# A later place for ScalarE's evacuation of the product with V, and a power of two moved into the exponential's bias

## The chip, the cores and the metric

The kernel runs on one core of a Trainium2 chip. The metric is the device time of one execution in microseconds. Times are compared by medians of runs; the rows below come from one profiled execution.

## The reference

The program computes pooled attention and then an MLP with a layer norm, in float32. q, k and v have 4 batches, 8 heads, 1152 positions and 64 columns. Pairs of query positions are averaged, so there are 576 queries per head.

```
q_pool = q.reshape(B, H, S // 2, 2, D).mean(axis=3)
scores = scale * q_pool @ k.T;  scores -= max(scores)
attn = exp(scores);  attn /= sum(attn) + 1e-9
x = attn @ v            # heads side by side: (4, 576, 512)
xn = (x - mean) / sqrt(var + 1e-6) * g_ln
out = x + max(xn @ w_ch1, 0) @ w_ch2
```

## The kernel before

**Tiles and steps.** Two heads of one batch make a pair; there are 16 pairs. Each pair has 9 tiles of 128 queries (the fifth holds 64 queries of either head), so there are 144 steps, one tile of 128 queries by 1152 keys each. The steps are written out by hand, in `step(i)`; every engine runs its instructions in the order in which they are written there. In the first 36 steps (`on_pe`) the exponentials are transposed by TensorE (PE) in float32. In the other 108, which the change is about, they are split into an fp16 high and low half and transposed by a DMA.

**A step i of the second kind**, in the order of writing:

- `emit_max(i)`: VectorE (DVE) takes the row maximum of the scores from PSUM (L381) and makes the bias `nb` of the exponential from it (L386).
- `emit_s(i + 1)`: PE computes the scores of the next tile (L362, and L370 for the last 128 keys). A tile of scores takes three PSUM banks, a slot; two slots alternate. L370 writes the third bank of a slot.
- `flush()`: what was put on the list `evacs` in the step before. First the two parts of `evac_pv`, which evacuate the product with V: `one` is DVE's sum and reciprocal `r` (L513, L514), `two` is ScalarE's (ACT's) scaled copy into the tile `xb` or `xh` (L524). Then the evacuation of the MLP unit (ACT's high half of `ht`, L618, and DVE's low half, L619; or DVE's residual add, L650), of the layer norm's transposes (L574, L575), and the high and low halves of the next pair's k and q (L286 or L311, and L283 or L306).
- `emit_exp(i)` and `emit_hi(i)`: ACT's exponential from PSUM into the SBUF tile `pe` (L395), and its high half into `hl` (L409), with the factor 2^15. Three buffers of `hl` are in turn; one is free again when its transposing DMA is done.
- `emit_lo(i - 1)`: the low half, (2^15 pe - hi), by DVE (L418), or for tiles 2, 5 and 8 of a pair (`low_on_pool`) by GpSimd (POOL) with one pass that scales `pe` in place (L251) and one that subtracts (L416). Then the DMA that transposes `hl` into `pt` (L421), on the queue of SP.
- `norm(i)`: the layer norm of a finished block of 128 rows: DVE's statistics (L550, L551) and POOL's scaling (L556 to L562).
- `a_piece(i)`: PE's product with V of a tile four steps back (L464). It goes into columns 128 to 257 of the third bank of the slot whose first 128 columns hold the last scores of step i + 1. Its evacuation is put on `evacs`.
- `some_units(i)`: one unit of the MLP, if there is one: PE's L605 (first matmul) or L637 (second). `a_prep`: one transpose of k or q for the next pair (L297, L301 or L325). Further transposes are those of the layer norm (L568). All of these take one of two PSUM banks from `bank()`. If neither is free, `bank()` calls `flush()` early, in the middle of the step.
- the end of the step: loads, ACT's Abs passes over k, q and v (`bound`, L185) in the second and third step of a pair, from whose sums PE, DVE and GpSimd make the scales of the next pair in the two steps after (`all_max`, `scales`).

After step 143 the MLP units that are left run on PE, two a step.

Of the kernel before, what the change touches and what calls it, by code (L numbers as in the profile page):

```python
# [2 lines left out]

# [10 lines left out]
ACTF = mybir.ActivationFunctionType  # L14
ALU = mybir.AluOpType
# [9 lines left out]
def tile_pooled_attention_moe(  # L25
# [18 lines left out]
    nc = tc.nc  # L44
# [4 lines left out]
    C = S // 128  # L49
# [178 lines left out]
    def scales(p, top, a=0, b=3, both=False):  # L228
        st = pair[p]
        red, e, s, sc = (st[x] for x in ("red", "e", "s", "sc"))  # L230
        v = nc.vector
        v.tensor_scalar(red[:, a:b], top, TINY, None, op0=ALU.max)
        if both:

            v.tensor_tensor(red[:, 0:1], red[:, 0:1], red[:, 2:3], op=ALU.max)
        ri, ei, si = (x.bitcast(I32)[:, a:b] for x in (red, e, s))
        v.tensor_scalar(ei, ri, EXPO, None, op0=ALU.bitwise_and)
        v.tensor_scalar(si, ri, EXPO, EXPO, op0=ALU.bitwise_and, op1=ALU.bitwise_xor)

        v.tensor_scalar(s[:, a:b], s[:, a:b], 2.0 ** 13, None, op0=ALU.mult)  # L240
        if a == 0:
            v.scalar_tensor_tensor(
                sc[:, 0:1], e[:, 0:1], 2.0 ** -32, e[:, 1:2], op0=ALU.mult, op1=ALU.mult
            )
            if on_pe(p * C):
                v.scalar_tensor_tensor(
                    sc[:, 1:2], e[:, 0:1], -(2.0 ** -32), e[:, 1:2], op0=ALU.mult, op1=ALU.mult
                )

    def scaled(dst, src, s=1.0):  # L250
        nc.gpsimd.tensor_scalar(dst, src, s, 1.0, op0=ALU.mult, op1=ALU.mult)  # L251
# [84 lines left out]
    def on_pe(i):  # L336

        return 0 <= i < HP * C

    def low_on_pool(i):  # L340
        return i % C in (2, 5, 8)
# [35 lines left out]
    def emit_max(i):  # L377
        st = steps[i]
        mx = sm_p.tile([128, 1], FP32, tag="mx", name="mx")
        nb = st["nb"] = sm_p.tile([128, 1], FP32, tag="nb", name="nb")  # L380
        nc.vector.tensor_reduce(mx, st["s"], axis=AX.X, op=ALU.max)  # L381
        sc = pair[i // C]["sc"]
        if on_pe(i):
            st["mx"] = mx
        else:
            nc.vector.tensor_scalar(nb, mx, sc[:, 0:1], -1.0, op0=ALU.mult, op1=ALU.mult)  # L386

    def emit_exp(i):
        st = steps[i]
# [16 lines left out]
    def emit_hi(i):  # L406
        st = steps[i]
        hl = st["hl"] = p_p.tile([128, 2, S], FP16, tag="hl", name="hl", bufs=3)
        nc.scalar.activation(out=hl[:, 0], in_=st["pe"], func=ACTF.Copy, scale=2.0 ** 15)  # L409

    def emit_lo(i):
        st = steps[i]
        hl = st["hl"]
        if low_on_pool(i):
            scaled(st["pe"], st["pe"], 2.0 ** 15)
            nc.gpsimd.tensor_tensor(hl[:, 1], st["pe"], hl[:, 0], op=ALU.subtract)  # L416
        else:
            nc.vector.scalar_tensor_tensor(  # L418
                hl[:, 1], st["pe"], 2.0 ** 15, hl[:, 0], op0=ALU.mult, op1=ALU.subtract
            )  # L420
        nc.sync.dma_start_transpose(out=pt_of(i), in_=hl.rearrange("p a n -> p (a n)"))  # L421
# [65 lines left out]
    def evac_pv(i, ps):  # L487

        p, j = divmod(i, C)
        b, hp = divmod(p, HP)  # L490
        s = pair[p]["s"][:, 2:3]
        r = sm_p.tile([128, 2], FP32, tag="r", name="r", bufs=3)
        if j == 4:
            if b % 2 == 0 and hp == 0:
                xh[b // 2] = x_p.tile([128, 2, DM], FP32, tag="hh", name="xh")
            o, n, m = 64 * (b % 2), 64, 2
            x = xh[b // 2][o:o + n, 0, 128 * hp:128 * hp + 128]
        else:
            if j == 0 and hp == 0:
                room["x"] -= 4  # L500
                assert room["x"] >= 0
                xb[b] = x_p.tile([128, 4, DM], FP32, tag="xb", name="xb")
            h, t = PLACES[hp // 2][j]
            o, n, m = 0, 128, 1
            x = xb[b][:, t, 128 * hp + 64 * h:128 * hp + 64 * h + 64]
        r = r[o:o + n, 0:m]

        def one():
            sums = ps[o:o + n, 64:65 * m:65]
            if on_pe(i):  # L510
                nc.vector.reciprocal(r, sums)
            else:
                nc.vector.tensor_scalar(r, sums, EPS, s[o:o + n], op0=ALU.add, op1=ALU.mult)  # L513
                nc.vector.reciprocal(r, r)  # L514

        def two():
            for u in range(m):
                if on_pe(i):
                    nc.vector.tensor_scalar(
                        x[:, 64 * u:64 * u + 64], ps[o:o + n, 65 * u:65 * u + 64],  # L520
                        r[:, u:u + 1], None, op0=ALU.mult,
                    )
                    continue
                nc.scalar.activation(  # L524
                    out=x[:, 64 * u:64 * u + 64], in_=ps[o:o + n, 65 * u:65 * u + 64],
                    func=ACTF.Copy, scale=r[:, u:u + 1],
                )

        return one, two
# [47 lines left out]


    units, preps = deque(), deque()
    evacs = []  # L580

    def flush():
        mine, evacs[:] = list(evacs), []
# [333 lines left out]
    def evacuated(n):  # L917

        p, j = divmod(n, C)
        b = p // HP  # L920
        left[p] -= 1
        if not left[p]:
            pair.pop(p)
        key = ("h", b // 2) if j == 4 else (b, PLACES[p % HP // 2][j][1])
        whole[key] = whole.get(key, 0) + 1
        if whole[key] == 8 and key != ("h", 0):
            norms.append(key)
# [17 lines left out]
    def a_piece(i):  # L945
        pieces.extend(ready.pop(i, ()))
        for u in range(2 if len(pieces) > 2 and not on_pe(i) else 1):
            if pieces:
                n = pieces.popleft()
                pt = pts[n]  # L950
                ps = emit_pv(n, bank() if u or on_pe(n) else None)
                if on_pe(n):
                    ot = pt.rearrange("p a n -> p (a n)").bitcast(FP32)[0:65, 0:128]
                    evacs.append(lambda ot=ot, ps=ps: nc.scalar.activation(
                        out=ot, in_=ps[0:65, 0:128], func=ACTF.Identity, bias=eps
                    ))
                    turned.append((n, ot))
                    continue
                evacs.extend(evac_pv(n, ps))
                evacs.append(lambda n=n: evacuated(n))  # L960

    def step(i):
        live = i < NSTEP
        this[0] = i
        for fn, a in early.pop(i, ()):
            fn(*a)
        if live:
            emit_max(i)
        if on_pe(i - 1):
            emit_t_copy(i - 1)  # L970
            steps.pop(i - 1)
        while found:
            found.popleft()()
        first = on_pe(i - 2) or on_pe(i)
        if first and not on_pe(i):
            a_piece(i)
        if on_pe(i):
            if i < 3:
                warm(16, bank())
            a_piece(i)  # L980
            a_prep()
            emit_exp(i)
        while scaled_out:
            scaled_out.popleft()()
        if i + 1 < NSTEP:
            emit_s(i + 1)
            pv_slot[0] = i + 1
        else:
            free_banks[:] = [6, 7, 0, 1, 3, 4]
            pv_slot[0] += 1  # L990
        if on_pe(i):
            while fill:
                drip()
            flush()
        else:
            flush()
            if live:
                emit_exp(i)
                emit_hi(i)
        if 0 <= i - 1 < NSTEP and not on_pe(i - 1):  # L1000
            emit_lo(i - 1)
            steps.pop(i - 1)
            drip()
        norm(i)
        while soon or len(fill) > 3:
            drip()
        if on_pe(i):
            emit_t(i)
            if reds:
                found.append(reds.popleft()())  # L1010
        elif reds:
            evacs.append(reds.popleft()())
        while turned:
            n, ot = turned.popleft()
            emit_turn(n, ot, i)
        if not on_pe(i):
            if not first:
                a_piece(i)
            some_units(i)
            a_prep()  # L1020
        for fn, a in todo.pop(i, ()):
            fn(*a)
        if calm and i < HP * C - 1:
            gate()
        for _ in range(1 if i < HP * C - 1 else 2):
            if calm:
                fn, n = calm.popleft()
                fn(n)
# [6 lines left out]
    with tc.manual_schedule():  # L1035
# [17 lines left out]
        st = state(0)  # L1053
# [29 lines left out]
        i = 0  # L1083
# [32 lines left out]
```

## Time and profile before

| what | value |
|---|---|
| runs | 865.6, 866.25, 870.39 us; median 866.25 |
| profiled execution | 860.85 us, its span 859.0 us |
| PE, DVE, ACT, POOL busy | 810.0, 604.2, 561.8, 349.5 us |
| TensorE's granted clock over the span | 0.996 of full speed |

The span is the time from the first to the last instruction of the profiled execution. Busy times are sums over it. A row of a timeline has the start of an instruction in us from the span's start, its duration in us, the engine, the line, the output and input by the program's names, and in brackets how long the engine had been idle and what ended that.

### The profile page before, as it was taken

The page shows a single profiled execution, that of the slowest core. Times are in us where ns is not written, and L with a number is a line of the kernel's source. Part 1 is how long each engine was busy: PE and PEld are TensorE (multiplying, and loading weights), DVE is VectorE, ACT ScalarE, POOL GpSimd, SP SyncE. Part 2 cuts the span into 40 slices and gives each one's busy share as a digit, 9 for nine tenths or more (in the row PEclk, how much of TensorE's full clock was granted, in tenths as well). Part 3 has the DMA queues.
Part 4 walks back from the last instruction along what each step waited for, and adds up shares of the span by engine and source line. Part 5 has one row for each costly group of instructions (what it writes and reads, how often), then busy time and mean ns, then how long its engine had stood idle before and what let it go on. Part 6 is the DMA issues. An engine that isn't in the chain of part 4 may idle for free.

```text
span 859.0 us, 21617 instructions
## 1 busy us (share of the span) xinstructions
PE 810.0 (94%) x9142; PEld 574.4 (67%) x9142; DVE 604.2 (70%) x1166; ACT 561.8 (65%) x810; POOL 349.5 (41%) x345
## 2 busy tenths in 40 slices
PE   7999999988889998998999999999999999999997
PEld 6787877766556665656575766666666666766764
DVE  4698899898778877788777777777777777531221
ACT  3999988867676767677686867676867676311110
POOL 3020333487888845436534244634542514300000
PEclk9999999999999999999999999999999999999999
DMA  6853465025695869887898989776989968500001
GB/s 178 223 206 122 158 179 182 1 63 107 134 203 110 175 124 223 147 166 141 156 180 158 174 146 203 146 153 123 217 143 158 171 117 139 100 10 20 19 2 24
DMA packets 276016, 115.95 MB, mean 135 GB/s; under 512 B 259280, under 2 KB 259280, under 8 KB 275920
## 3 DMA queue, kind: packets, MB, share of 16 engines
q1 hardware_dynamic: 275568, 113.70, 64.5%
q8 instruction: 71, 1.16, 0.6%
q10 hardware_dynamic: 352, 0.88, 0.4%
q14 instruction: 25, 0.20, 0.1%
HBM read 46.14 MB, written 4.72 MB: 59 GB/s over the span
## 4 chain that ended last, share of the span: by engine, by line
PE 45%; DVE 27%; ACT 12%; DMA 8%; issue 4%; POOL 2%; SPq 2%; ACTq 0%; POOLq 0%; DVEq 0%
PE psum L637 14%; PE psum L605 14%; DVE mx L381 8%; DVE hl L418 6%; PE psum L464 5%; PE psum L362 4%; ACT pe L395 3%; DMA qr<-in_q_dram 2%; DMA kr<-in_k_dram 2%; DVE ht L619 2%; PE psum L452 2%; ACT ht L618 2%; DMA pt<-hl 2%; DVE kt L283 2%; PE psum L428 2%
## 5 line engine op out<-in xcount | busy, mean ns | idle before, releaser
L381 DVE TENSOR_REDUCE mx<-psum 128x1 f32<-128x1152 f32 x144 | 194.7, 1352 | 19.3 <-ACT xb L524 7.4
L637 PE MATMUL psum<-wsl,ht 128*128 128x512 f16 x864 | 196.6, 379 | 5.1 <-DVE ht L619 4.3
L395 ACT ACTIVATE pe<-psum,nb,sc 128x1152 f32<-128x1152 f32 x144 | 188.8, 1311 | 11.8 <-DVE nb L386 10.4
L605 PEld LDWEIGHTS <-wsl 128*128 128x128 f16 x1920 | 170.2, 98 | 28.2 <-issue 9.6
L605 PE MATMUL psum<-xn,wsl 128*128 128x256 f16 x1536 | 178.1, 274 | 8.8 <-DVE xb L650 5.9
L637 PEld LDWEIGHTS <-ht 128*128 128x128 f16 x864 | 80.8, 98 | 93.6 <-issue 5.8
L409 ACT ACTIVATE hl<-pe 128x1152 f16<-128x1152 f32 x108 | 125.6, 1163 | 9.5 <-DMA pt<-hl 6.2
L362 PE MATMUL psum<-kt,qt 64*128 64x512 f16 (+1 forms) x960 | 127.3, 380 | 1.9 <-ACT pe L395 0.9
L619 DVE SCALAR_TENSOR_TENSOR ht<-psum,ht 128x512 f16<-128x512 f32 x72 | 49.8, 692 | 100.7 <-ACT ht L618 100.7
L464 PE MATMUL psum<-vt,pt 128*128 128x65 f16 (+1 forms) x3240 | 118.4, 194 | 0.2 <-DMA pt<-hl 0.2
L418 DVE SCALAR_TENSOR_TENSOR hl<-pe,hl 128x1152 f16<-128x1152 f32 x72 | 112.1, 1556 | 0.0
L464 PEld LDWEIGHTS <-pt 128*128 128x128 f16 (+1 forms) x3240 | 110.1, 101 | 2.8 <-DMA pt<-hl 0.7
L618 ACT ACTIVATE ht<-psum 128x512 f16<-128x512 f32 x72 | 42.7, 593 | 87.0 <-PE psum L605 86.6
L251 POOL TENSOR_SCALAR pe<-pe 128x1152 f32<-128x1152 f32 x36 | 43.1, 1198 | 130.5 <-ACT hl L409 130.5
L524 ACT ACTIVATE xb<-psum,r 128x64 f32<-128x64 f32 x96 | 29.9, 311 | 93.8 <-DVE r L514 80.6
L416 POOL TENSOR_TENSOR hl<-pe,hl 128x1152 f16<-128x1152 f32 x36 | 85.5, 2374 | 3.0
L452 PE MATMUL psum<-pt,vt 128*65 128x128 f32 (+1 forms) x720 | 77.4, 263 | 1.1 <-DVE qt L283 1.1
L452 PEld LDWEIGHTS psum<-pt,vt 128*65 128x65 f32 x720 | 71.5, 138 | 1.3 <-DVE qt L283 1.3
L362 PEld LDWEIGHTS <-qt 64*128 64x128 f16 (+1 forms) x960 | 39.7, 96 | 39.6 <-issue 22.1
L370 PEld LDWEIGHTS <-qt 128*128 128x128 f16 (+1 forms) x320 | 17.0, 99 | 61.5 <-issue 61.4
L283 DVE SCALAR_TENSOR_TENSOR qt<-psum,s,qt 128x384 f16<-128x384 f32 x48 | 29.5, 615 | 31.1 <-ACT qt L286 31.0
L257 POOL COPY gate<-gate 128x1 f32<-128x1 f32 x27 | 5.2, 193 | 110.5 <-DVE gate L256 110.5
(116 smaller groups left out, 1010.8 us busy)
## 6 DMA issues: line engine op xcount, KB each, us to landing
stage<-in_moe_w_ch_dram SPq DMA_DIRECT2D x32, 512.0 KB, 5.9
kr<-in_k_dram SPq DMA_DIRECT2D x16, 576.0 KB, 4.6
qr<-in_q_dram SPq DMA_DIRECT2D x31, 288.0 KB, 6.1
vr<-in_v_dram SPq DMA_DIRECT2D x15, 576.0 KB, 5.0
out_dram<-xb SPq DMA_DIRECT2D x32, 128.0 KB, 2.4
pt<-hl SPq DMA_TRANSPOSE x108, 4.9
kr<-in_k_dram SPq DMA_DIRECT2D x16, 64.0 KB, 4.2
vr<-in_v_dram ACTq DMA_DIRECT2D x1, 576.0 KB, 6.5
```

Source lines behind the costliest of these rows:

```text
L362: nc.tensor.matmul(out=sp[o:o + w, c0:c0 + 512], lhsT=qt[r:r + 64, qa, q0:q0 + w], rhs=kt[r:r + 64, ka, h], start=(a == 0), stop=(a == 2),)
L381: nc.vector.tensor_reduce(mx, st["s"], axis=AX.X, op=ALU.max)
L395: nc.scalar.activation(out=st["pe"], in_=st["s"], func=ACTF.Exp, scale=pair[i // C]["sc"][:, 0:1], bias=st["nb"],)
L409: nc.scalar.activation(out=hl[:, 0], in_=st["pe"], func=ACTF.Copy, scale=2.0 ** 15)
L416: nc.gpsimd.tensor_tensor(hl[:, 1], st["pe"], hl[:, 0], op=ALU.subtract)
L418: nc.vector.scalar_tensor_tensor(hl[:, 1], st["pe"], 2.0 ** 15, hl[:, 0], op0=ALU.mult, op1=ALU.subtract)
L452: nc.tensor.matmul(out=ps[0:65, q0:q0 + w], lhsT=vt[:, h, c], rhs=pt[:, 128 * u + q0:128 * u + q0 + w], start=(u == 0), stop=(u == C - 1),)
L464: nc.tensor.matmul(out=dst[:, 0:n], lhsT=lhsT, rhs=rhs, start=(u == 0 and lhsT is hi and n == 65), stop=(u == C - 1 and lhsT is lo), skip_ ...
L605: nc.tensor.matmul(out=ps[:, o:o + n], lhsT=wsl[:, 8 * w + cc, wa, f * 128:f * 128 + 128], rhs=xn[:, xa * KD + cc, 0:n], start=(m == 0), s ...
L618: lambda: nc.scalar.activation(out=hi, in_=pv, func=ACTF.Relu),
L619: lambda: nc.vector.scalar_tensor_tensor(lo, pv, 0.0, hi, op0=ALU.max, op1=ALU.subtract),
L637: nc.tensor.matmul(out=ps, lhsT=hv[0][:, ha, f, t * 128:t * 128 + 128], rhs=wsl[:, 8 * w + 4 + f // 2, wa, (f % 2) * DM:(f % 2) * DM + DM] ...
```

## The change

Three edits. The second part of the evacuation of the product with V (L524) is no longer put on `evacs` but on a list of its own, `last`. A step takes that list at its start and runs it behind the exponential and the high half, ahead of the low half; the first part stays on `evacs`. Second, for GpSimd's tiles the bias of the exponential gets 15 log 2 added, so that `pe` itself is 2^15 times as large; the high half is then taken with the factor 1, and GpSimd's pass that scaled `pe` is left out. Third, `nb` is made with the negative product of the scales and an addition, so `scales` makes that product for every pair and not only for the first four.

```diff
--- before.py
+++ after.py
@@ -1,3 +1,4 @@
+import math
 from collections import deque
 from contextlib import ExitStack
 
@@ -242,10 +243,9 @@
             v.scalar_tensor_tensor(
                 sc[:, 0:1], e[:, 0:1], 2.0 ** -32, e[:, 1:2], op0=ALU.mult, op1=ALU.mult
             )
-            if on_pe(p * C):
-                v.scalar_tensor_tensor(
-                    sc[:, 1:2], e[:, 0:1], -(2.0 ** -32), e[:, 1:2], op0=ALU.mult, op1=ALU.mult
-                )
+            v.scalar_tensor_tensor(
+                sc[:, 1:2], e[:, 0:1], -(2.0 ** -32), e[:, 1:2], op0=ALU.mult, op1=ALU.mult
+            )
 
     def scaled(dst, src, s=1.0):
         nc.gpsimd.tensor_scalar(dst, src, s, 1.0, op0=ALU.mult, op1=ALU.mult)
@@ -383,7 +383,8 @@
         if on_pe(i):
             st["mx"] = mx
         else:
-            nc.vector.tensor_scalar(nb, mx, sc[:, 0:1], -1.0, op0=ALU.mult, op1=ALU.mult)
+            up = 15 * math.log(2) if low_on_pool(i) else 0.0
+            nc.vector.tensor_scalar(nb, mx, sc[:, 1:2], up, op0=ALU.mult, op1=ALU.add)
 
     def emit_exp(i):
         st = steps[i]
@@ -406,13 +407,13 @@
     def emit_hi(i):
         st = steps[i]
         hl = st["hl"] = p_p.tile([128, 2, S], FP16, tag="hl", name="hl", bufs=3)
-        nc.scalar.activation(out=hl[:, 0], in_=st["pe"], func=ACTF.Copy, scale=2.0 ** 15)
+        up = 1.0 if low_on_pool(i) else 2.0 ** 15
+        nc.scalar.activation(out=hl[:, 0], in_=st["pe"], func=ACTF.Copy, scale=up)
 
     def emit_lo(i):
         st = steps[i]
         hl = st["hl"]
         if low_on_pool(i):
-            scaled(st["pe"], st["pe"], 2.0 ** 15)
             nc.gpsimd.tensor_tensor(hl[:, 1], st["pe"], hl[:, 0], op=ALU.subtract)
         else:
             nc.vector.scalar_tensor_tensor(
@@ -577,7 +578,7 @@
 
 
     units, preps = deque(), deque()
-    evacs = []
+    evacs, last = [], []
 
     def flush():
         mine, evacs[:] = list(evacs), []
@@ -956,8 +957,9 @@
                     ))
                     turned.append((n, ot))
                     continue
-                evacs.extend(evac_pv(n, ps))
-                evacs.append(lambda n=n: evacuated(n))
+                one, two = evac_pv(n, ps)
+                evacs.append(one)
+                last.extend((two, lambda n=n: evacuated(n)))
 
     def step(i):
         live = i < NSTEP
@@ -972,6 +974,7 @@
         while found:
             found.popleft()()
         first = on_pe(i - 2) or on_pe(i)
+        final, last[:] = list(last), []
         if first and not on_pe(i):
             a_piece(i)
         if on_pe(i):
@@ -997,6 +1000,8 @@
             if live:
                 emit_exp(i)
                 emit_hi(i)
+        for fn in final:
+            fn()
         if 0 <= i - 1 < NSTEP and not on_pe(i - 1):
             emit_lo(i - 1)
             steps.pop(i - 1)
```

## Rows read from the trace of the kernel before

**Rows 1.** The page, busy us of the engines, share of the span, instructions

```profile
PE 810.0 (94%) x9142; PEld 574.4 (67%) x9142; DVE 604.2 (70%) x1166; ACT 561.8 (65%) x810; POOL 349.5 (41%) x345
```

**Rows 2.** The page, chain of work that ended last, by engine

```profile
PE 45%; DVE 27%; ACT 12%; DMA 8%; issue 4%; POOL 2%; SPq 2%; ACTq 0%; POOLq 0%; DVEq 0%
```

**Rows 3.** Busy us by stretch: length, PE, PEld, DVE, ACT, POOL, clock, DMA

```profile
220.00:400.00 180.00, 161.49 (x1996) 107.34 (x1996) 139.03 (x244) 126.13 (x169) 115.16 (x93) 0.98 0.84 162
400.00:740.00 340.00, 330.92 (x4193) 224.12 (x4190) 257.49 (x470) 242.86 (x322) 144.57 (x130) 1.00 0.86 156
```

**Rows 4.** Instructions of L409: ns min/median/max, first and last start

```profile
L409 ACT ACTIVATE hl<-pe x108: 1162/1163/1166, 186.3 to 734.5; 128x1152 f16<-128x1152 f32 x108
```

**Rows 5.** Waits of PE: us in total, times, longest

```profile
PE psum L605 <- DVE xb L650: 5.9, 4, 2.1
PE psum L637 <- DVE ht L619: 4.3, 5, 1.0
PE psum L605 <- DVE ht L619: 2.9, 4, 1.7
...
PE psum L370 <- DVE xb L519: 0.7, 2, 0.4
```

**Rows 6.** Waits of the other engines: us in total, times, longest

```profile
DVE ht L619 <- ACT ht L618: 100.7, 71, 3.4
...
ACT xb L524 <- DVE r L514: 80.6, 65, 5.9
...
DVE mx L381 <- ACT xb L524: 7.4, 11, 1.7
...
ACT hl L409 <- DMA pt<-hl: 6.2, 7, 2.8
```

**Rows 7.** Timeline of a step: start, us, engine, line, names [idle before, releaser]

```profile
450.84 0.38 PE L301 MATMUL psum<-ident,kr 128*128 128x128 f32 x2
...
451.84 0.21 DVE L513 TENSOR_SCALAR r<-psum,s 128x1 f32<-128x1 f32 x1
...
452.03 0.98 PE L464 MATMUL psum<-vt,pt 128*128 128x65 f16 x27
...
452.35 0.32 ACT L524 ACTIVATE xb<-psum,r 128x64 f32<-128x64 f32 x1 [1.92 <-DVE r L514]
452.56 0.59 ACT L618 ACTIVATE ht<-psum 128x512 f16<-128x512 f32 x1
...
453.18 0.69 DVE L619 SCALAR_TENSOR_TENSOR ht<-psum,ht 128x512 f16<-128x512 f32 x1 [0.93 <-ACT ht L618]
...
453.92 2.75 PE L637 MATMUL psum<-wsl,ht 128*128 128x512 f16 x12 [0.91 <-DVE ht L619]
```

**Rows 8.** Timeline from 272 to 300 us, where DVE is late

```profile
283.57 0.51 ACT L524 ACTIVATE xh<-psum,r 64x64 f32<-64x64 f32 x2 [3.43 <-DVE r L514]
...
284.72 0.62 DVE L283 SCALAR_TENSOR_TENSOR qt<-psum,s,qt 128x384 f16<-128x384 f32 x1 [1.25 <-ACT qt L286]
...
293.21 2.78 PE L605 MATMUL psum<-xn,wsl 128*128 128x256 f16 x24 [1.90 <-DVE xb L650]
```

**Rows 9.** Timeline from 308 to 345 us, a high half that waits for its buffer

```profile
334.39 0.28 PE L370 MATMUL psum<-kt,qt 128*128 128x128 f16 x2
...
334.95 1.16 ACT L409 ACTIVATE hl<-pe 128x1152 f16<-128x1152 f32 x1 [2.83 <-DMA pt<-hl]
```

**Rows 10.** L418 and GpSimd's passes: groups of the page, then ns min/median/max

```profile
L418 DVE SCALAR_TENSOR_TENSOR hl<-pe,hl 128x1152 f16<-128x1152 f32 x72 | 112.1, 1556 | 0.0
...
L251 POOL TENSOR_SCALAR pe<-pe 128x1152 f32<-128x1152 f32 x36 | 43.1, 1198 | 130.5 <-ACT hl L409 130.5
...
L418 DVE SCALAR_TENSOR_TENSOR hl<-pe,hl x72: 1347/1350/3510, 189.3 to 733.9; 128x1152 f16<-128x1152 f32 x72
...
L251 POOL TENSOR_SCALAR pe<-pe x36: 1149/1153/2248, 199.8 to 737.9; 128x1152 f32<-128x1152 f32 x36
```

## Prediction

> **What bounds the kernel now.** I read the page's busy times first: PE is busy 810.0 us of a span of 859.0 [rows 1], so all idle time of PE is worth 49 us at most. The chain that ended last says where it lies: 45% PE, 27% DVE, 12% ACT [rows 2]; DVE's queue often released what came last, even where PE had other work. The busy times by stretch narrow it: from 220 to 400 us PE is idle 18.5 us of 180, from 400 to 740 us 9.1 us of 340 [rows 3]. The steps that the change touches run their high half from 186.3 to 734.5 us, 108 of them [rows 4], so about 30 us of PE idle lie inside its reach, and most of the second stretch is pure PE.
>
> The list of what PE waited for tells which idle it is [rows 5]: 4.3 us ahead of the second MLP matmul and 2.9 us ahead of the first, both for the low half of `ht` (L619) that frees a PSUM bank; 5.9 us for the residual add L650. On the other engines [rows 6]: DVE sat idle 100.7 us, 71 times (1.42 us each), ahead of L619 for the high half of `ht` from ACT, and ACT sat idle 80.6 us, 65 times, ahead of the evacuation `xb` (L524) for the reciprocal of DVE. These two are one story, and one step shows it [rows 7]: the MLP unit's matmuls are over when the transposes of L301 begin, 450.84. ACT stands idle 1.92 us, because the next in its queue is `xb`, which needs `r`, which stands on DVE behind the maximum and `nb`. Only after `xb` (452.35) come `ht` (452.56) and the kt copy; so DVE gets to L619 at 453.18, and PE, through with its product with V at 452.03 + 0.98 = 453.01, waits 0.91 us until 453.92.
>
> **The change, part by part.**
>
> *`xb` behind the high half.* In such a step ACT now runs `ht` as soon as the unit's matmuls are over, about 450.9 to 451.5, and kt after it. DVE has `r` at 451.84 + 0.21 and the reciprocal some 0.2 us later, about 452.25, and goes straight into L619, 0.69 us, to 452.94. That is before 453.01, so the 0.91 us go whole. Nine waits of PE are of this kind (7.2 us, rows 5). Eight of them end on the step's order, and I take all of them; in the ninth, the largest of L605 (1.67 us, the first step after the change of scheme), the scale work ahead of `r` stays and 0.9 us go. Sum: 7.2 - 0.8 = 6.4 us.
>
> The DVE chain gets shorter too. At 283.57 ACT had waited 3.43 us for `r` ahead of the evacuation; the copy of the queries was queued behind it, and DVE stood 1.25 us for that copy. DVE is late in that stretch, and PE pays at 293.21 with 1.90 us for L650 [rows 8]. There I take 1.2 us, DVE's whole wait. The other waits for L650 start from a maximum that waits for its scores or behind a stretched low half; 1.0 us of them in all, mostly because the maximum no longer waits for `xb` where an early flush puts `xb` ahead of it (7.4 us, 11 times, rows 6). Together 2.2 us.
>
> What pays: (a) behind `xb` ACT runs the Abs passes L185 in two steps of each pair, and PE waits for these. ACT does the same work in another order; where it was saturated nothing changes, where a high half waits for its buffer the passes come 0.3 us later. I take 0.3 us once; bounds 0 and 12 pairs x 0.3 = 3.6. (b) The layer norm's statistics read `xb`. In nine steps they now stand on DVE until the high half and `xb` are through, up to 1.2 us each, and the next maximum is queued behind them. PE has no gap behind them in those steps, and DVE has idle time in the next; I take 0, bounds 0 and 9 x 0.5 = 4.5. (c) A new wait: the scores of step i+2 write the third bank of the slot that `xb` reads (L370), so PE there waits for exp, high half and `xb` and no longer for exp alone. Behind L370 are queued the product with V and the next unit. Normally L370 begins 0.7 us or more after the high half's end; where the high half waits for its buffer (6.2 us, 7 times, rows 6) it doesn't: at 334.95 it starts after 2.83 us of waiting, ends 336.11, and with 0.31 of `xb` L370 goes from 334.39 to some 336.45 [rows 9]. Just behind it PE has one of its waits for L650, which swallows most; 0.3 us left there, 0.2 us at a second such place. Bounds: 0, and the worst case of the slower rival below.
>
> Is that wait real, since `xb` and L370 touch different columns? The rows speak for it: the maximum, which reads other columns of the bank, waited for `xb` [rows 6], and L370 waited twice for a DVE evacuation, 0.7 us [rows 5]. By the same rows exp keeps waiting for `r`, whose sum DVE reads from the bank, and not for `nb` alone; so I count no gain for exp itself. The Trainium skill (PSUM — Partial Sum Buffer, "PSUM bank collisions raise a hardware error") speaks against the change here: two engines must not be in one bank on the same partitions at once, reads against reads included, and the guard goes by bank, not by address. By that rule L370 stands behind `xb` in all 108 steps, which is the slower rival's mechanism; if waits went by columns, (c) would cost nothing and the sum be -8.0 us. The trace agrees as far as these two rows go.
>
> *2^15 through the bias.* 36 passes of GpSimd go, 1198 ns on average, 43.1 us; its subtraction can start when ACT's high half ends, so the low half and its transposes come 1.2 us earlier. PE hardly waits for any transposed tile in these steps, so nothing on the path. What could gain is DVE: its low half takes 1347 ns at the least and 3510 at the most, 112.1 us for 72, so 15 us of stretch [rows 10], which lies beside GpSimd's work. The passes are 43.1 of GpSimd's 349.5 us [rows 1]: 12% of 15 is 1.8 us. They seldom meet the low half, though: a median of 1153 against a mean of 1198 ns is 1.6 us of stretch over all 36 passes. I take 0, bounds -1.8, and +1.8 if the subtraction, now earlier, meets more of DVE's work. The bias itself goes into an instruction that is there (`nb`, mult and add in place of two mults), and ACT's scale is 1 in place of 2^15: 0.
>
> *One more scale product in 12 pairs*: of the size of `r`, 0.21 us [rows 7], and queued ahead of it: 2.5 us if all on the path; PE is mostly busy there, 0.3 taken.
>
> **Sum**: -6.4 - 2.2 + 0.3 + 0.5 + 0.3 = -7.5 us. The profiled execution took 860.85 us, of which 1.85 lie around the span: 853.4. The median of the runs is 866.25, 5.4 higher; the same step from there gives 858.7.
>
> **Rivals.**
>
> *The gaps only move.* PE is busy 97% of the second stretch; a step that is ready sooner meets the next limit (the maximum behind a late low half, the loads of q and k). For it: the waits for L650 that start from a late maximum, for L185's sums and for the layer norm's transposes stay where they are. Against: PE has 9.1 us of idle time in the whole second stretch, so few waits are there to take it back. If half is given back: -3.5, 862.7.
>
> *DVE sets more of the pace than I count.* It has 27% of the chain, and loses most of 100.7 us of waiting. Then the rest of the waits for L650 (5.9 less 2.2) and a like amount of the other idle time before 400 us go as well: 7 us more, -14.5, 851.7. Against: from 400 us on only 9.1 us are there to be had.
>
> *Slower, by the third bank.* L370 held behind high half and `xb` is one mechanism; it decides where the high half ends later than L370's start less 0.4 us. If all seven buffer waits fall through to PE they cost 6.2 + 7 x (1.16 + 0.31) = 16.5 us, and only the gaps behind them cover it: +16.5 - 8 = +8.5 at worst, +6 taken, 872. For it: 334.95 [rows 9]. Against: the other six waits share 3.4 us, and L370 stands later there.
>
> *It doesn't do what it says*: where the unit is unfinished when DVE has `r`, the order of the two makes no difference. That happens in other steps, not in the nine counted; it ends with the first rival.
>
> **Chances.** Forecast 0.55 (its own range 853 to 862, as the bounds will not all fall on one side); gaps move or nothing happens 0.23; DVE's pace 0.13; slower 0.09. This kernel's runs lie within 0.6%, so 0.5% (4.3 us) is about what can be told from no change: faster 0.68, same 0.23, slower 0.09. The range, 849 to 866, leaves out the slower rival and the far end of the faster one.
>
> **What would show it.** The wait of `xb` for the reciprocal gone from ACT's list, L619's wait for `ht` well under 100 us; PE's waits for L619 ahead of L605 and L637 near zero; the maximum never waiting for `xb`. A new row "L370 waits for `xb`" would show (c): under 3 us in sum if I am right, over 8 if the slower rival is. The statistics L550 should wait for `xb`. GpSimd busy about 306 us, and the low half's longest times as before. I am wrong if those waits go and PE's idle from 220 to 740 us stays near 27 us, or if it falls under 15.

## The result, and the profile after

The changed kernel took 852.79 us (median of 6 runs, 847.55 to 857.0), the kernel before 864.66 beside it (862.87 to 870.39): a ratio of 0.9861, 95% interval 0.9819 to 0.9903. In a second measurement it was 850.92 against 863.46, ratio 0.9866 (0.9833 to 0.9899). So the change gains 1.3 to 1.4%, some 12 us; forecast were 7.5. The sign and the range hold, the size is 4 to 5 us short.

The time of one kernel goes with the mean granted clock of its run: 846.89 us at 1.0 and 855.91 at 0.989 in the second measurement, 858.78 at 1.0 and 867.62 at 0.989 for the kernel before. The first profiled run of the changed kernel was its slowest (857.0, clock 0.990). All lines of the changed kernel below are therefore from the profiled run of the second measurement (849.85, span 848.1, clock 0.995). Lines behind the edits stand one or two lower than before: L201 is now L202, L409 is L411, L418 L419, L524 L525, L568 L569, L605 L606, L618 and L619 are L619 and L620, L637 L638, L650 L651.

The page of that run: the busy times, and the chain of work that ended last, by engine.

```profile
PE 808.2 (95%) x9142; PEld 574.1 (68%) x9142; DVE 606.1 (71%) x1178; ACT 558.1 (66%) x810; POOL 308.5 (36%) x309
...
PE 64%; ACT 11%; DVE 11%; DMA 6%; issue 4%; SPq 1%; POOL 1%; ACTq 0%; POOLq 0%; DVEq 0%
```

DVE gained 12 small instructions (the scale products) and stayed as busy; GpSimd lost its 36 passes, 41 us. The chain changed from 45% PE and 27% DVE [rows 1, 2] to 64% and 11% (63% and 11% in the first profiled run): DVE's queue seldom releases the work that came last any more.

Busy times by stretch, columns as in [rows 3], with GB/s behind the DMA share:

```profile
220.00:400.00 180.00, 164.84 (x2077) 110.92 (x2078) 146.19 (x258) 129.15 (x173) 104.98 (x85) 0.98 0.86 165
400.00:735.00 335.00, 329.17 (x4174) 222.69 (x4172) 255.52 (x474) 236.88 (x321) 117.22 (x107) 1.00 0.87 160
```

PE's idle time from 220 us on is 15.2 + 5.8 = 21.0 us, against 18.5 + 9.1 = 27.6 [rows 3]. I had called the forecast wrong if it stayed near 27 or fell under 15. In the first profiled run, at its lower clock, the two stretches hold 15.7 + 8.3 = 24.0 us. Over the whole span idle time went from 859.0 - 810.0 = 49.0 to 848.1 - 808.2 = 39.9 us.

PE's waits, us in total, times, longest:

```profile
PE psum L202 <- ACT kt L186: 6.4, 6, 2.0
...
PE psum L569 <- DVE ht L620: 4.1, 4, 1.1
PE psum L370 <- ACT xb L525: 3.3, 5, 1.4
...
PE psum L606 <- DVE xb L651: 2.3, 2, 1.9
...
PE psum L606 <- DVE ht L620: 0.7, 1, 0.7
```

And those of the other engines that answer to [rows 6]:

```profile
ACT ht L619 <- PE psum L606: 131.9, 59, 12.4
DVE ht L620 <- ACT ht L619: 86.4, 59, 3.5
...
ACT pe L396 <- DVE r L514: 9.8, 10, 2.2
...
ACT hl L411 <- DMA pt<-hl: 9.6, 11, 2.4
...
DVE bs L551 <- ACT xb L525: 8.5, 9, 1.9
...
ACT xb L525 <- DVE r L515: 8.1, 2, 4.6
```

The second MLP matmul (L638) no longer waits for anything that the list shows; the first waits once for `ht`. ACT's 80.6 us ahead of `xb` are 8.1, in two places. The maximum never waits for `xb`. What appeared is what the forecast named: exp waits for `r`, L370 for `xb`, the statistics L551 for `xb`. One sign came only in part: L620 still waits 86.4 us of 100.7 for `ht`, since `ht`, no longer behind `xb`, now waits for its own matmul in more places (131.9 us, 59 times; 86.6, 29 times before).

The step of [rows 7], 7.0 us earlier on this kernel's clock:

```profile
443.81 0.38 PE L301 MATMUL psum<-ident,kr 128*128 128x128 f32 x2
444.00 0.60 ACT L619 ACTIVATE ht<-psum 128x512 f16<-128x512 f32 x1 [1.07 <-PE psum L606]
...
444.66 0.21 DVE L514 TENSOR_SCALAR r<-psum,s 128x1 f32<-128x1 f32 x1
...
444.98 0.67 DVE L620 SCALAR_TENSOR_TENSOR ht<-psum,ht 128x512 f16<-128x512 f32 x1
445.00 0.98 PE L465 MATMUL psum<-vt,pt 128*128 128x65 f16 x27
...
445.81 2.75 PE L638 MATMUL psum<-wsl,ht 128*128 128x512 f16 x12
...
447.31 0.30 ACT L525 ACTIVATE xb<-psum,r 128x64 f32<-128x64 f32 x1
```

`ht` now waits for its own matmul (1.07 us) and for nothing else; `xb` comes 3.3 us after it. From the transposes L301 to the second MLP matmul it takes 445.81 - 443.81 = 2.00 us, where it took 453.92 - 450.84 = 3.08 [rows 7]: 1.08 us less, forecast 0.91. The low half L620 starts when PE starts its product with V, and ends before that does.

### The profile page after: what moved, and what is told of

The parts are those of the page before. It is cut to its first block, busy times and chain, and to the rows that moved or that the text cites. A ratio compares the mean times of both kernels' runs of the same rounds, so it can differ in the third digit from the quotient of the medians.

```text
span 855.2 us, 21585 instructions
## 1 busy us (share of the span) xinstructions
PE 811.9 (95%) x9142; PEld 577.1 (67%) x9142; DVE 603.0 (71%) x1178; ACT 558.8 (65%) x810; POOL 308.5 (36%) x309
## 4 chain that ended last, share of the span: by engine, by line
PE 63%; ACT 11%; DVE 11%; DMA 8%; issue 3%; SPq 2%; POOL 1%; ACTq 0%; POOLq 0%; DVEq 0%
PE psum L606 19%; PE psum L638 18%; PE psum L465 9%; PE psum L362 7%; ACT pe L396 4%; DVE mx L381 3%; DMA qr<-in_q_dram 3%; DMA pt<-hl 3%; PE psum L453 2%; PE psum L370 2%; DMA kr<-in_k_dram 2%; ACT kt L186 2%; PE psum L429 1%; PE psum L325 1%; ACT pt L435 1%
## 5 line engine op out<-in xcount | busy, mean ns | idle before, releaser
L638 PE MATMUL psum<-wsl,ht 128*128 128x512 f16 x864 | 196.6, 379 | 0.0
L606 PEld LDWEIGHTS <-wsl 128*128 128x128 f16 x1920 | 170.5, 99 | 20.9 <-issue 1.7
L606 PE MATMUL psum<-xn,wsl 128*128 128x256 f16 x1536 | 179.6, 276 | 1.1 <-DVE ht L620 0.7
L638 PEld LDWEIGHTS <-ht 128*128 128x128 f16 x864 | 80.4, 98 | 87.8
L417 POOL TENSOR_TENSOR hl<-pe,hl 128x1152 f16<-128x1152 f32 x36 | 88.2, 2451 | 137.9 <-ACT hl L411 137.9
L411 ACT ACTIVATE hl<-pe 128x1152 f16<-128x1152 f32 x108 | 125.6, 1163 | 14.1 <-DMA pt<-hl 10.9
L619 ACT ACTIVATE ht<-psum 128x512 f16<-128x512 f32 x72 | 42.9, 595 | 135.0 <-PE psum L606 133.1
L620 DVE SCALAR_TENSOR_TENSOR ht<-psum,ht 128x512 f16<-128x512 f32 x72 | 49.6, 689 | 92.3 <-ACT ht L619 92.2
L419 DVE SCALAR_TENSOR_TENSOR hl<-pe,hl 128x1152 f16<-128x1152 f32 x72 | 111.0, 1542 | 0.0
L453 PE MATMUL psum<-pt,vt 128*65 128x128 f32 (+1 forms) x720 | 79.0, 266 | 1.1 <-DVE qt L283 1.1
L453 PEld LDWEIGHTS psum<-pt,vt 128*65 128x65 f32 x720 | 73.0, 140 | 1.3 <-DVE qt L283 1.3
L362 PEld LDWEIGHTS <-qt 64*128 64x128 f16 (+1 forms) x960 | 39.9, 96 | 38.8 <-issue 22.4
L370 PEld LDWEIGHTS <-qt 128*128 128x128 f16 (+1 forms) x320 | 17.6, 99 | 67.0 <-issue 66.8
L651 DVE SCALAR_TENSOR_TENSOR xb<-psum,inv,xb 128x512 f32<-128x512 f32 x32 | 23.9, 747 | 37.1 <-PE psum L638 36.0
L286 ACT ACTIVATE qt<-psum,s 128x384 f16<-128x384 f32 x48 | 27.7, 578 | 32.9 <-PE psum L325 32.8
L435 ACT COPY pt<-psum 128x512 f32<-128x512 f32 x72 | 44.6, 639 | 6.2 <-PE psum L481 2.7
```

Source lines behind the costliest of these rows:

```text
L362: nc.tensor.matmul(out=sp[o:o + w, c0:c0 + 512], lhsT=qt[r:r + 64, qa, q0:q0 + w], rhs=kt[r:r + 64, ka, h], start=(a == 0), stop=(a == 2),)
L419: nc.vector.scalar_tensor_tensor(hl[:, 1], st["pe"], 2.0 ** 15, hl[:, 0], op0=ALU.mult, op1=ALU.subtract)
L435: nc.scalar.copy(st["pt"][:, a:b], st["s"][:, a:b])
L453: nc.tensor.matmul(out=ps[0:65, q0:q0 + w], lhsT=vt[:, h, c], rhs=pt[:, 128 * u + q0:128 * u + q0 + w], start=(u == 0), stop=(u == C - 1),)
L606: nc.tensor.matmul(out=ps[:, o:o + n], lhsT=wsl[:, 8 * w + cc, wa, f * 128:f * 128 + 128], rhs=xn[:, xa * KD + cc, 0:n], start=(m == 0), s ...
L620: lambda: nc.vector.scalar_tensor_tensor(lo, pv, 0.0, hi, op0=ALU.max, op1=ALU.subtract),
```

## The experiments

Three questions: which half of the change pays; whether `xb` must stand where it was put; and what the changed kernel still loses by the waits that it got. Each run was timed beside the kernel before; the ratio of a run is to that, with its 95% interval in brackets.

**Which half.** The changed kernel again, as the base of this group.

> The changed kernel once more, beside the others on the same chip. Theory (the copy xb no longer holds back ACT's high half of ht): 8 to 12 us under the kernel before at whatever clock is granted. Rival (the gain is TensorE's clock, which was granted higher in these runs): runs of both kernels at the same mean granted clock differ by under 4 us.

850.92 us, ratio 0.9866 (0.9833 to 0.9899), 12.5 us under the kernel before: the first result stands. The rival falls: at a granted clock of 1.0 the two kernels took 846.89 and 858.78 us, at 0.989 855.91 and 867.62, which is 11.9 and 11.7 us apart.

Then the move of `xb` alone, GpSimd's pass and ACT's factor left as before:

```diff
-                evacs.extend(evac_pv(n, ps))
-                evacs.append(lambda n=n: evacuated(n))
+                one, two = evac_pv(n, ps)
+                evacs.append(one)
+                last.extend((two, lambda n=n: evacuated(n)))
...
+        final, last[:] = list(last), []
...
+        for fn in final:
+            fn()
```

> Only the move of xb; GpSimd's scaling pass, the bias and the scales as before. Theory: all but about 1 us of the gain, 7 to 11 us under the kernel before. Rival (GpSimd's pass held up DVE's low halves and the transposes): under half of it, 0 to 5 us.

853.4 us, 0.9891 (0.9862 to 0.992), 10.1 us under the kernel before. Its PE waits are those of the whole change:

```profile
PE psum L201 <- ACT kt L185: 6.9, 5, 2.3
...
PE psum L370 <- ACT xb L524: 3.3, 3, 1.5
...
PE psum L605 <- DVE xb L650: 2.6, 2, 2.0
...
PE psum L605 <- DVE ht L619: 0.6, 1, 0.6
```

And the bias alone, with `xb` back in its old place:

```diff
-                one, two = evac_pv(n, ps)
-                evacs.append(one)
-                last.extend((two, lambda n=n: evacuated(n)))
+                evacs.extend(evac_pv(n, ps))
+                evacs.append(lambda n=n: evacuated(n))
```

> Only GpSimd's pass goes, with the bias and one more scale product in 12 pairs; xb stays ahead of ht. Theory: 2 us faster to 1 us slower than the kernel before, PE still waits some 7 us for the low half of ht. Rival (GpSimd's pass): 5 us faster or more.

861.16 us (12 runs), 0.9979 (0.9961 to 0.9996), 2.3 us under the kernel before. The waits of [rows 5] and [rows 6] are back, all of them:

```profile
DVE ht L620 <- ACT ht L619: 104.7, 71, 3.2
...
ACT xb L525 <- DVE r L515: 80.6, 64, 4.7
...
DVE mx L381 <- ACT xb L525: 7.8, 11, 1.7
```

```profile
PE psum L606 <- DVE xb L651: 4.6, 4, 1.7
PE psum L638 <- DVE ht L620: 4.1, 5, 0.9
...
PE psum L606 <- DVE ht L620: 3.0, 4, 1.7
```

So the move carries 1.1% and makes the changes of the waits shown above; the bias carries 0.2%, barely clear of nothing. The two add up: 10.1 + 2.3 = 12.4 us against the 12.5 measured for both.

**Where `xb` must stand.** If the gain comes from `ht` getting out from behind `xb`, it does not matter where behind `ht` the evacuation stands. Between exp and high half:

```diff
                 emit_exp(i)
-                emit_hi(i)
         for fn in final:
             fn()
+        if live and not on_pe(i):
+            emit_hi(i)
```

> As the changed kernel, but xb between the exponential and its high half, so that it no longer stands behind a high half that waits for a buffer. If the new waits of the last score product (L370) for xb, 5.3 us in the changed kernel's profile, cost time: those waits under 1 us and 1 to 4 us faster than the changed kernel. If they only lie where PE would have waited anyway (behind it for L651, or for the Abs sums): within 1 us of the changed kernel.

850.26 us, 0.9853 (0.9826 to 0.9881): 0.7 us from the changed kernel with no wait of L370 for `xb` left, the second of the two cases. Then ahead of exp, as the last of what the step evacuates:

```diff
             flush()
+            for fn in final:
+                fn()
             if live:
...
-        for fn in final:
-            fn()
```

> As the changed kernel, but xb stands behind ht and the k and q copies and still ahead of the exponential. Theory (what counts is that the copies of the MLP and of k and q leave ACT ahead of xb; the exponential and the high half need not): 10 to 13 us under the kernel before, L370's waits for xb gone. Rival (the gain is the exponential's, which no longer waits for the reciprocal and for xb): 5 to 8 us under the kernel before.

851.77 us, 0.9858 (0.9828 to 0.9889), 11.6 us under the kernel before, and L370's waits for `xb` are gone, as the theory has it. And the sharpest form: `xb` keeps its place ahead of the k and q copies, exp and the high half, and only `ht` goes ahead of it.

```diff
-        final, last[:] = list(last), []
...
-        for fn in final:
-            fn()
...
             some_units(i)
+            evacs.extend(last)
+            del last[:]
             a_prep()
```

> As the changed kernel, but in ACT's queue only the evacuation of the MLP unit (ht) goes ahead of xb; the copies of k and q, the exponential and the high half stay behind it, and an early flush takes xb along as before. If PE's nine waits for the low half of ht make the gain: 7 to 9 us under the kernel before, with the waits of L606 and L638 for L620 gone. If the shorter chain of DVE (copies of k and q, the maximum not held by xb) makes more of it than I counted: 4 to 7 us under, the rest missing.

850.19 us, 0.9844 (0.9814 to 0.9875), 14.0 us under the kernel before: more than either expectation, 7 to 9 or 4 to 7. Nor did all nine waits go. Two are left, 0.7 us ahead of L606 at 212 us and 0.9 ahead of L638 at 218, soon after the change of scheme:

```profile
PE psum L638 <- DVE ht L620: 0.9, 1, 0.9
...
PE psum L606 <- DVE ht L620: 0.7, 1, 0.7
```

The counterpart of the step above, in this kernel:

```profile
445.29 0.38 PE L301 MATMUL psum<-ident,kr 128*128 128x128 f32 x2
445.49 0.60 ACT L619 ACTIVATE ht<-psum 128x512 f16<-128x512 f32 x1 [1.07 <-PE psum L606]
...
446.47 0.67 DVE L620 SCALAR_TENSOR_TENSOR ht<-psum,ht 128x512 f16<-128x512 f32 x1
...
446.58 0.31 ACT L525 ACTIVATE xb<-psum,r 128x64 f32<-128x64 f32 x1 [0.50 <-DVE r L515]
...
447.30 2.75 PE L638 MATMUL psum<-wsl,ht 128*128 128x512 f16 x12
```

ACT still idles 0.50 us ahead of `xb` for the reciprocal, and from L301 to L638 it takes 2.01 us, as in the changed kernel. ACT's list has 43.9 us of such waits left, in 41 places:

```profile
ACT xb L525 <- DVE r L515: 43.9, 41, 4.2
```

Four orders, one gain, within their intervals. What pays is that `ht` does not stand behind an evacuation that waits for DVE; the place behind the high half is one way to that, and 44 us of ACT waiting for DVE cost nothing that can be measured. Why this form gained 14.0 us where 7 to 9 were expected stays open: in its profile PE's waits sum to 35.0 us, 8.6 less than the 43.6 of the kernel before.

**What the change still loses.** Three waits of the changed kernel were taken away. First the wait for the Abs sums L186 (L202, 6.4 us): PE's transpose of these sums stood in its queue ahead of the product with V; it is put behind it.

```diff
-        elif reds:
-            evacs.append(reds.popleft()())
...
                 a_piece(i)
+            if reds:
+                evacs.append(reds.popleft()())
             some_units(i)
```

> The changed kernel with one more edit: PE's transpose of the Abs sums (L202, 6.4 us of waits, up to 2.0 each) stands behind the product with V, 0.98 us, in place of ahead of it. If these waits are on the path: 2 to 5 us faster than the changed kernel. If the next maximum, which needs the same bank, only waits in their place: within 1 us of it.

846.59 us, 0.9806 (0.9777 to 0.9836): the largest of the single steps, about 0.6% on top of the change, though the two intervals still touch (0.9833). Its wait:

```profile
PE psum L202 <- ACT kt L186: 2.1, 2, 1.1
```

Second, the high half's wait for its buffer (9.6 us): four buffers of `hl` in place of three, the space taken from a staging buffer and small tiles.

```diff
-        hl = st["hl"] = p_p.tile([128, 2, S], FP16, tag="hl", name="hl", bufs=3)
+        hl = st["hl"] = p_p.tile([128, 2, S], FP16, tag="hl", name="hl", bufs=4)
...
-            st = raw_p.tile([128, 512, 2], I32, tag="stage", name="stage", bufs=2)
+            st = raw_p.tile([128, 512, 2], I32, tag="stage", name="stage", bufs=1)
```

> The changed kernel with four buffers of hl in place of three (room taken from one of two buffers for loads of the weights, whose turn is shifted, and from small tiles). ACT's waits of the high half for a buffer, 9.6 us, under 3, and L370's for xb, 3.3 us, under 1. If they are on the path: 1 to 4 us faster than the changed kernel; if they are covered by what PE waits for anyway: within 1 us.

849.32 us, 0.984 (0.9809 to 0.9872). L411 does not wait for its buffer any more, and L370's wait falls with it:

```profile
PE psum L370 <- ACT xb L525: 0.6, 1, 0.6
```

Its interval overlaps that of the change alone (0.9866): a gain of at most a few us, not told apart from none. Third, both orders together, `xb` between exp and high half and the sums later:

> xb between the exponential and the high half, and the transpose of the Abs sums behind the product with V. If both act by themselves: 3 to 6 us faster than the changed kernel, some 846 us; if they draw on the same idle time: 1 to 2 us.

846.25 us, 0.98 (0.977 to 0.9831), as the later sums alone (its edit is the two above). All three edits together (the order of `xb`, the later sums, four buffers):

> xb between the exponential and the high half, the transpose of the Abs sums behind the product with V, and four buffers of hl. If the three draw on different idle time: 843 to 846 us, 2.1 to 2.4% under the kernel before; if the buffers add nothing once xb no longer stands behind the high half: 846 to 847.

844.07 us (runs of 842.52 to 845.58), 0.9778 (0.9747 to 0.9809): the fastest version, 2.2% under the kernel before, and its interval lies wholly under that of the change alone (0.9833 to 0.9899). Its chain is PE for three quarters:

```profile
PE 74%; DVE 9%; ACT 8%; DMA 5%; issue 2%; POOL 1%; SPq 1%; ACTq 0%; POOLq 0%; DVEq 0%
```

## Why the prediction was right, and its size short

**`xb` behind the high half: right, and to the size.** The nine waits of PE ahead of the MLP's matmuls for the low half, 7.2 us [rows 5], are 0.7 us in one place. Forecast -6.4, measured -6.5. That one is the ninth, at 212 us, of which I had kept 0.8. The bias alone leaves all nine, the move alone leaves one of 0.6 us, and the kernel in which only `ht` goes ahead leaves two, 1.6 us of the 7.2, with the gain whole. So it is shown that `ht` behind `xb` is the cause of the gain; how the part of it beyond these waits comes about is not.

The layer norm's transposes wait for the same low half, and there the list shows 4.1 us where it showed 2.1. These are lines of the kernel before:

```profile
PE psum L568 <- DVE ht L619: 2.1, 2, 1.1
...
PE psum L568 <- POOL vt L251: 1.1, 1, 1.1
PE psum L568 <- POOL pe L251: 1.0, 1, 1.0
```

The time did not grow: the four waits are the same ones, 1.0 to 1.1 us each, two of them put down to GpSimd before. All waits of these transposes together are 7.4 us before and 7.3 after. The change doesn't touch them.

**The shorter DVE chain: -4.1 in place of -2.2, and part of that only changed its name.** PE's waits for the residual add were 5.9 + 0.8 + 0.4 = 7.1 us (L605, L637, L568) and are 2.3 of `xb`, with 0.3 and 0.4 us of `xh` left beside them: 3.0. I allowed DVE's whole wait (1.2 us) at 293.21 and then only 1.0 us for the rest, since those start from a maximum that waits for its scores. In the counterpart of 293.21 PE waits 0.41 us, 1.49 less:

```profile
290.69 2.78 PE L606 MATMUL psum<-xn,wsl 128*128 128x256 f16 x24 [0.41 <-DVE xb L651]
```

Most of the other gain stands in the step of [rows 9], where I had foreseen an exchange. Before, PE waited there for the residual add:

```profile
337.51 2.67 PE L605 MATMUL psum<-xn,wsl 128*128 128x256 f16 x23 [1.61 <-DVE xb L650]
```

Now it waits for `xb`, ahead of L370, and the MLP unit behind it starts without a wait:

```profile
332.68 0.27 PE L370 MATMUL psum<-kt,qt 128*128 128x128 f16 x2 [1.43 <-ACT xb L525]
...
333.61 2.78 PE L606 MATMUL psum<-xn,wsl 128*128 128x256 f16 x24
```

So this term and (c) are to be read together: forecast -2.2 + 0.5 = -1.7, measured -4.1 + 3.3 = -0.8 (-0.7 in the first profiled run, -0.5 with the move alone). The size fell short elsewhere. In the version with only `ht` ahead these waits stay at 4.5 us and L370's wait for `xb` is gone, at the same time as the whole change; PE's waits sum to 35.0 us there and to 34.6 in the changed kernel.

**(a) The Abs passes, forecast +0.3:** PE's wait for them went from 7.7 to 6.4 us in one run and to 8.4 in the other, so nothing to tell. **(b) The statistics:** they stand for `xb` nine times, 8.5 us, as foretold, and nothing in PE's list follows; between exp and high half that wait falls to 1.4 us and the time hardly moves.

**(c) The third bank, forecast +0.5:** the wait is real, five times, 3.3 us (5.3 in the first profiled run), at or over the 3 us that I had set as the end of "right", and far from the 8 of the slower rival. Most of it is covered, though: with no such wait (between exp and high half) the kernel takes 850.26 against 850.92, 0.7 us less and within the intervals. As the price in the sum 0.5 was fair, as the size of the row it was low. The columns read differ from those written, and PE waits all the same; exp waits ten times for `r`, 9.8 us, though of what DVE makes in the step it needs `nb` alone. The Trainium skill (PSUM — Partial Sum Buffer, "PSUM bank collisions raise a hardware error") says that the guard goes by bank and holds for reads against reads; these two rows agree with it. They are waits for the program's semaphores; what an access without them would do no run here shows. By that rule L370 stands behind `xb` in all 108 steps; it has to wait in 5, because in the others PE gets to L370 0.3 us or more after `xb` has ended.

**2^15 through the bias: taken as 0, and it is not.** Alone it gains 0.2% (0.04 to 0.39), some 2.3 us (0.3 to 3.4): the middle is just outside my bound of -1.8, the interval holds it. On top of the move it is 2.5 us (853.4 to 850.92), which by itself the intervals do not tell from nothing. Where it lies the profiles do not settle. PE's list of waits sums to 43.7 us with the bias alone and to 43.6 before. DVE's low half, which I had named as the place, took 109.5 us with the bias alone against 112.1 [rows 10], but 113.8 with both edits:

```profile
L419 DVE SCALAR_TENSOR_TENSOR hl<-pe,hl 128x1152 f16<-128x1152 f32 x72 | 113.8, 1580 | 0.0
```

So less stretch of DVE is not shown to be the cause, and the cause of these 2.3 us stays open.

**The account.** In the second profiled run PE's idle time is 9.1 us less and its busy time 1.8 us less, 10.9 in all. The idle time by PE's waits: -6.5 for `ht` ahead of the MLP, -4.1 for the residual add, +3.3 for `xb` at L370, -1.8 in all the rest; forecast were -6.4, -2.2, +0.5, +0.6. So the three terms of the move that can be read from waits gave -7.3 where I had -8.1; what I had too small is the rest, and the 1.8 us of busy time that I did not price. The runs say the same by halves. The move alone was forecast at -8.1 + 0.3 = -7.8 us and measured at -10.1, interval 6.9 to 11.9, so its size is not told apart from the forecast. The bias with its scale products was forecast at 0 + 0.3 and measured at -2.3: this is the term that was sized wrong, by 2.6 of the 4 to 5 us.

**The rivals.** "The gaps only move" fell: the lead over the kernel before, by the start of the same maximum, is 2.2 us at its 248 us, 6.2 at 375, 8.2 at 495, 10.2 at 730. It is given back for a while in places, down to 0.1 us at 259, behind the lower clock of the last section, and by some 2 us at 545 and 726, and it comes again. "DVE sets more of the pace" has the nearer time, 851.7 us, and DVE's share of the chain fell from 27% to 11%; its mechanism is not borne out, since PE's idle time fell by 9.1 us in all, not by the 14.5 that it needed, and DVE lost only 14 of the 100.7 us of waiting for `ht`, not most of them. "Slower by the third bank" fell with (c).

## What to carry to other kernels

In an in-order queue ask of each instruction what stands behind it that could already run, and put the one that waits for another engine last among those; whether the engine itself then waits less is beside the point, since 44 us of ACT waiting for DVE cost nothing measurable once `ht` was ahead. Price a reorder by the waits of the bound engine that it ends, but add those further down the chain of the queue that gets free (here 4.1 us beside 6.5), and set against these the new waits by the PSUM bank where an evacuation is put later (here 3.3). When a change leaves one wait standing in the bound engine's own queue (the transpose of the Abs sums ahead of a product that was ready), moving that is worth a run of its own: it gave 0.6% more, at the edge of the intervals.

## What the runs showed that I had not expected

Two of the remaining waits of the changed kernel stand close together, and the clock falls behind them:

```profile
247.73 0.30 PE L370 MATMUL psum<-kt,qt 128*64 128x128 f16 x4 [1.00 <-ACT xb L525]
...
250.02 0.38 PE L202 MATMUL psum<-ident,acc 128*3 128x128 f32 x1 [1.99 <-ACT kt L186]
...
251.67 4.86 PE L606 MATMUL psum<-xn,wsl 128*128 128x256 f16 x24
```

```profile
247.70:251.60 3.90, 1.89 (x31) 1.66 (x31) 0.87 (x3) 3.90 (x6) 3.82 (x3) 0.68 1.16 234
251.60:256.50 4.90, 4.90 (x31) 3.34 (x30) 2.25 (x6) 1.42 (x3) 2.72 (x3) 0.56 0.86 160
```

PE is busy 1.89 us of 3.90; the granted clock is 0.68 in this stretch and 0.56 in the next (mostly the lower level, 1.2 GHz, of the two, 1.2 and 2.4), and a unit of 24 matmuls that takes 2.78 us elsewhere takes 4.86, 2.1 us more. The kernel before has a dip at this place too, to 0.68 in the same 4.9 us. With the sums later the product with V fills the gap, and the clock stays at full level:

```profile
247.70:251.60 3.90, 2.90 (x53) 1.91 (x51) 2.39 (x6) 3.90 (x8) 3.90 (x3) 1.00 1.25 227
251.60:256.50 4.90, 4.90 (x64) 3.82 (x63) 4.64 (x9) 4.28 (x6) 4.19 (x4) 1.00 1.15 142
```

From 240 to 260 us the two stretches of 10 us hold a clock of 0.66 to 0.86 in one of them in all nine profiles without this edit, and of 1.00 in both in the three profiles with it. So a wait of PE can cost more than its length. The later sums beat the change by 4.3 us (846.59 against 850.92): L202's wait is 4.3 us shorter, this stretch is gone, and three other waits of PE grew by 0.7 to 0.8 us each (L453, L481, and L370 for DVE). Over the runs of one kernel 0.011 of mean granted clock goes with 9 us (855.91 against 846.89), three quarters of what the change gains; a comparison of the first profiled executions alone (857.0 against 860.85, 3.85 us) would have hidden two thirds of what the medians show.
